# The last cast and the output store, moved from VectorE and SyncE to ScalarE

## The chip, the cores and the metric

The kernel runs on one core of a Trainium2 chip. The metric is device time in microseconds (us). The profile also gives a span, from the first to the last instruction of the program; it is about 1.8 us shorter than the time (1327.8 against 1329.5 us in the profiled run of the kernel before).

Lengths below a tenth of a microsecond are read from the records of single instructions, semaphore updates and DMA packets in the trace. The views round to 0.01 us, and the span to 0.1 us.

## The reference, cut to what matters

```
def reference(A_x, A_k_cache, A_v_cache, A_wq, A_wo, B_x, B_w1, ..., gate_w):
    # A: one decode step of attention, B=2, H=32, Sk=16384, Dh=128, all bf16
    q = (x @ wq) ...; scores = einsum(q, k_cache) * Dh**-0.5
    o = einsum(softmax(scores), v_cache);  a = o @ wo          # wo: 4096 x 1024
    # B: a small MLP on the same two rows
    b = x1 + gelu(layernorm(x1) @ w3) @ w4
    g = sigmoid((x * gate_w).sum(-1, keepdims=True))
    return g * a + (1 - g) * b                                 # 2 x 1 x 1024, bf16
```

The two caches are 537 MB; the result is 4 KB. The last thing that can happen is the product with `wo`, then the rounding of the sum to bf16, then the store.

## The kernel before

SyncE's queue carries every load of cache and weights. The last weight, `A_wo`, is cut into seven pieces, the last ones small, so that little work is left after the last byte. The sums of both halves of the model collect in one tile of PSUM (the memory that matmuls write to), `out_acc`.

```
    WO_SPLIT = [8, 8, 8, 4, 2, 1, 1]
    ...
    load_x()                          # two small loads, the only DMAs on ScalarE's queue
    ...
    wo = load_pieces(next_slot(), 0, A_wo, WO_SPLIT, ...)      # R.sync.dma_start, 7 pieces
    ...
    st_down(w4)
    wo_stage(wo)                      # matmuls into out_acc, piece by piece
    rows = t_tile([P, QW], BF16)
    R.vector.tensor_copy(out=rows, in_=out_acc)
    R.sync.dma_start(
        out=out.rearrange("b s (g n) -> g (b s) n", g=NQ),
        in_=rows[0 : P : APART, :],
        lane=(row_in[0], 32),
    )
    ...
    with tc.tile_critical(sync_engine=mybir.EngineType.Activation):
        R.emit([op for op in R.ops[:first_part] if op is not None])
        ...                           # the loops over the heads
        R.emit([op for op in R.ops[first_part:] if op is not None])
        nc.sync.wait_ge(row_in[0], 32)
```

`R` records operations and works out the semaphores between engines; all that it emits has the helper's line, L82, in the profile. The program must wait until the store has landed (`wait_ge`). And the section that holds the whole program is closed by one engine, named by `sync_engine`: here ScalarE ("Activation").

Of the kernel before, what the change touches and what calls it, by code (L numbers as in the profile page):

```python
# [184 lines left out]
def kernel(  # L185
# [15 lines left out]
    nc = tc.nc  # L201
# [19 lines left out]
    R = Order(nc, tc)  # L221
# [43 lines left out]
    def t_tile(shape, dtype, n=None):  # L265

        if n is None:
            n = t_next[0] % 2
            t_next[0] += 1
        flat = t_bufs[n][:]  # L270
        if dtype != FP32:
            flat = flat.bitcast(dtype)
        return shaped(flat, shape)
# [23 lines left out]
    def load_pieces(t, c0, weights, split, lanes, waits=()):  # L297
# [22 lines left out]
        out=perm[:].rearrange("k (h a) -> k h a", a=4),  # L320
        in_=ident_f[:].rearrange("k (a h) -> k h a", a=4),
# [23 lines left out]
    for g in range(1, 4):  # L345
        R.vector.tensor_tensor(
            out=osel_f, in0=osel_f, in1=ident_f[:, 40 * g : 40 * g + 8], op=ALU.add
# [9 lines left out]
        out=pick[:], in_=ident_f[:].rearrange("p (g w) -> p g w", w=32)[:, :, 0:B]  # L357
# [275 lines left out]
    out_acc = acc_ps[:, 0:QW]  # L633
# [203 lines left out]
    row_in = [tc.alloc_semaphore(f"row_in{n}") for n in range(2)]  # L837
# [33 lines left out]
    for k in range(LAST + 1):  # L871
# [19 lines left out]
    st_down(w4)  # L891
    wo_stage(wo)
    rows = t_tile([P, QW], BF16)
    R.vector.tensor_copy(out=rows, in_=out_acc)
    R.sync.dma_start(
        out=out.rearrange("b s (g n) -> g (b s) n", g=NQ),
        in_=rows[0 : P : APART, :],
        lane=(row_in[0], 32),
# [24 lines left out]
    def pe_loop():  # L923
        pe = nc.tensor
        got = Count(pe, sem["to_pe"])

        def scores(t):
            for m in range(NM):
                for v in range(4):
                    ins = score(pe, m, v)  # L930
                    if v == 0:
                        got.next(ins)
                    if v == 3:
                        ins.then_inc(sem["to_dve"], 1)

        def outputs(t):
            take(pe, v_in[t], 16)
            for m in range(NM):
                for g in range(4):
                    ins = weigh(pe, v_slot[t], m, g)  # L940
                    if m == 0 and g == 0:
                        ins.then_inc(sem["to_pool"], 1)
            ins.then_inc(sem["to_dve"], 1)
            got.next(join_heads(pe)).then_inc(sem["to_dve"], 1)

        def softmax(t):
            got.next(sum_rows(pe, mall, mdiag)).then_inc(sem["to_dve"], 1)
            got.next(sum_rows(pe, tot, stat["rs2"][:])).then_inc(sem["to_dve"], 1)
            take(pe, sem["from_pool"], 1)

        with pe.Fori(0, LAST + 1, NBIG) as k:
            loop_body(pe, k < LAST, scores, outputs, softmax, got.take_off)

    def dve_loop():
        dve = nc.vector
        counts = got, mine, exp_done = [
            Count(dve, sem[n]) for n in ("to_dve", "own_dve", "from_act")
        ]

        def scores(t):  # L960
            take(dve, k_in[t], 16)
            for m in range(NM):
                ins = turn_k(dve, k_slot[t + 1], m)
                if m >= 2:
                    got.next(ins)
                ins.then_inc(sem["to_pe"], 1)
            got.skip(1)
            got.next(top(dve)).then_inc(sem["own_dve"], 1)
            mine.next().then_inc(sem["free"], 1)

        def outputs(t):
            got.next(pick_head(dve, 0)).then_inc(sem["own_dve"], 1)
            for x in range(1, 4):
                mine.next(pick_head(dve, x)).then_inc(sem["own_dve"] if x < 3 else sem["to_pe"], 1)
            got.next(put_head(dve, bass.DynSlice(place + G * t, G))).then_inc(sem["free"], 1)

        def softmax(t):
            spread_top(dve).then_inc(sem["to_pe"], 1)
            got.next(head_top(dve, 0))
            head_top(dve, 1).then_inc(sem["own_dve"], 1)  # L980
            mine.next(bias(dve)).then_inc(sem["to_act"], 1)
            exp_done.next(turn_p(dve))
            split_sums(dve).then_inc(sem["to_pe"], 1)
            got.next(invert(dve))

        def take_off():
            for c in counts:
                if c.n:
                    c.take_off()

        with dve.Fori(0, G * (LAST + 1), G * NBIG) as place:
            loop_body(dve, place < G * LAST, scores, outputs, softmax, take_off)
# [17 lines left out]
    def act_steps():  # L1010
        for k in range(LAST + 1):
            exps(nc.scalar)._wait_ge(sem["to_act"], k + 1).then_inc(sem["from_act"], 1)

    def pool_steps():
        for k in range(LAST + 1):
            build_z(nc.gpsimd, min(k + 2, NT - 1))._wait_ge(sem["to_pool"], k + 1).then_inc(
                sem["from_pool"], 1
            )

    def meet(value):  # L1020
        for e in COMPUTE:
            getattr(nc, e).drain().then_inc(sem["met"], 1)
        for e in COMPUTE:
            getattr(nc, e).wait_ge(sem["met"], value)

    R.resolve()
    with tc.tile_critical(sync_engine=mybir.EngineType.Activation):
        R.emit([op for op in R.ops[:first_part] if op is not None])
        meet(len(COMPUTE))
        pe_loop()  # L1030
        dve_loop()
        act_steps()
        pool_steps()
        meet(2 * len(COMPUTE))
        R.emit([op for op in R.ops[first_part:] if op is not None])
        nc.sync.wait_ge(row_in[0], 32)


# [28 lines left out]
```

## Time and profile before

| | before |
|---|---|
| median time at first, 3 runs | 1329.58 us (1329.50 to 1329.78) |
| span of the profiled run | 1327.8 us |
| bytes read from HBM, mean rate | 572.5 MB, 431 GB/s |
| busy PE, DVE, ACT | 60%, 57%, 2% |
| last DMA of `A_wo` to the end of the span | about 4 us |

These lines are from the page of the kernel before. A digit of the DMA row is the mean busy share of the 16 DMA engines in one fortieth of the span, in tenths; 9 is 90% or more. The HBM line closes the list of DMA queues.

```profile
DMA  9999999999999999999999999999999999999998
...
HBM read 572.53 MB, written 0.00 MB: 431 GB/s over the span
```

The DMA engines are full from the first slice to the last but one. No compute engine is above 60%. So the time is that of the stream.

The next lines end the chain of work that ended last, in order of time (start, length, what).

```profile
1279.52 44.26 DMA slot<-in_A_wo_dram
1323.78 0.04 issue
1323.83 0.42 PE out_acc L82 x3
1324.27 0.42 DVE T L82
```

The chain sits on the transfer of `A_wo` for 44 us, and leaves it only for three matmuls and the cast. What follows is the tail that the change touches. The timeline of the kernel before shows it (start, length, engine, operation; in brackets, idle time of the engine before and what ended it):

```profile
1323.83 0.39 PE L82 MATMUL out_acc<-slot,T 128*17 128x256 bf16 x4 [0.23 <-DMA slot<-in_A_wo_dram]
1324.27 0.42 DVE L82 CAST T<-out_acc 128x256 bf16<-128x256 f32 x1 [16.30 <-PE out_acc L82]
1324.72 0.70 SPq L82 DMA_DIRECT2D out_dram<-T  x1
```

And the waits of SyncE's queue, where L1027 is the close of the program:

```profile
SPq L1027 <- DMA out_dram<-T: 1.0, 1, 1.0
```

The last matmuls end at 1324.2, the cast at 1324.7, the issue of the store at 1325.4, and SyncE waits 1.0 us for the landing. The rest to 1327.75 is closing synchronisation. In this document the **tail** is from the start of the cast to the end of the span, 3.48 us, and the **close** is its last part, from the landing of the store (the last update of its semaphore) to the end of the span, 1.29 us.

### The profile page before, as it was taken

Reading aid. Unit: us, or ns where it says so; the run is one execution under the profiler, and the core shown is the slowest. Engines: PE = TensorE matmul, PEld = TensorE weight load, DVE = VectorE, ACT = ScalarE, POOL = GpSimd, SP = SyncE. Lnnn points to the kernel's source line nnn. Section 1 sums busy time; section 2 is a strip of 40 time slices with the busy share of each in tenths; the row PEclk is TensorE's granted clock in tenths of the full one; section 3 lists DMA queues with packets and bytes.
Section 4 is the critical chain, followed back from the end, with each engine's and each line's share of the span. In section 5 each row is a group of like instructions: output and inputs, shape, how many; then the busy total and the mean of one; then the engine's idle time right before and its main releaser. Section 6 shows DMA issues by size and latency. Waiting matters only on the chain. (4 is left out here: it accounts for less than half of the span.)

```text
span 1327.8 us, 11371 instructions
## 1 busy us (share of the span) xinstructions
PE 801.6 (60%) x4806; PEld 305.4 (23%) x4859; DVE 762.7 (57%) x1009; ACT 27.2 (2%) x68; POOL 13.2 (1%) x41
## 2 busy tenths in 40 slices
PE   2767766555566655555765555576655557665553
PEld 1212222122222222222221222222222222222222
DVE  2277676655557665555666555566655556665540
ACT  0000000000000000000000000000000000000000
POOL 0000000000000000000000000000000000000000
PEclk9698887777888877778887777888777788877776
DMA  9999999999999999999999999999999999999998
GB/s 406 443 431 429 433 439 432 434 428 442 432 434 428 442 430 436 428 442 426 438 430 441 426 440 430 440 426 436 434 440 426 436 434 440 426 436 434 440 419 357
DMA packets 11118, 572.70 MB, mean 431 GB/s; under 512 B 1239, under 2 KB 1247, under 8 KB 1634
## 3 DMA queue, kind: packets, MB, share of 16 engines
q1 hardware_dynamic: 11100, 572.53, 99.6%
q8 instruction: 8, 0.13, 0.0%
q14 instruction: 4, 0.03, 0.0%
q10 hardware_dynamic: 6, 0.01, 0.0%
HBM read 572.53 MB, written 0.00 MB: 431 GB/s over the span
## 5 line engine op out<-in xcount | busy, mean ns | idle before, releaser
L526 PE MATMUL S<-T,z 128*128 128x512 bf16 x1933 | 571.6, 426 | 310.7 <-DVE T L517 298.8
L517 DVE STREAM_TRANSPOSE T<-slot 128x1024 f32<-128x1024 f32 x496 | 593.2, 1229 | 247.6 <-DVEq L921 196.0
L526 PEld LDWEIGHTS S<-T,z 128*128 128x128 bf16 x1984 | 171.1, 104 | 698.0 <-DVE T L517 532.5
L577 PE MATMUL O<-slot,PT 128*32 128x512 bf16 x2048 | 119.6, 387 | 7.2 <-PEq L921 7.2
L577 PEld LDWEIGHTS O<-slot,PT 128*32 128x32 bf16 x2048 | 74.0, 140 | 52.2 <-issue 23.0
L588 DVE TENSOR_SCALAR mix<-O,xmask 128x128 f32<-128x128 f32 x32 | 11.2, 351 | 103.6 <-PE O L577 103.6
L543 PE MATMUL tot<-rs,ones_f 128*128 128x2 f32 x62 | 18.2, 363 | 76.4 <-DVE rs L568 76.4
L560 ACT ACTIVATE mix<-S,nb 128x512 bf16<-128x512 f32 x31 | 21.3, 687 | 1158.3 <-DVE nb L550 1158.3
L596 PE MATMUL oc<-asel,mix 128*128 128x2 f32 x64 | 12.3, 262 | 51.8 <-DVE mix L591 51.8
L535 DVE TENSOR_REDUCE m<-S 128x1 f32<-128x512 f32 x31 | 21.4, 691 | 36.3 <-PE S L526 36.3
L565 DVE STREAM_TRANSPOSE PT<-mix 128x512 bf16<-128x512 bf16 x31 | 22.0, 711 | 26.2 <-ACT mix L560 26.2
L591 DVE SCALAR_TENSOR_TENSOR mix<-O,xmask,mix 128x128 f32<-128x128 f32 x96 | 33.7, 351 | 3.4
L543 PEld LDWEIGHTS tot<-rs,ones_f 128*128 128x128 f32 x62 | 15.5, 311 | 82.3 <-DVE rs L568 82.3
L543 PE MATMUL mall<-mix,ones_f 128*128 128x128 f32 x62 | 15.1, 326 | 16.3 <-DVE mix L538 16.3
L596 PEld LDWEIGHTS oc<-asel,mix 128*128 128x128 f32 x64 | 9.5, 188 | 66.2 <-DVE mix L591 66.2
L547 DVE TENSOR_REDUCE mx<-mall 64x1 f32<-64x64 f32 x62 | 13.8, 222 | 18.4 <-PE mall L543 18.0
L82 PE MATMUL out_acc<-slot,T 128*17 128x256 bf16 x240 | 12.1, 361 | 17.1 <-DMA slot<-in_A_wo_dram 9.3
L508 POOL TENSOR_TENSOR z<-qsel,own 128x32 bf16<-128x32 bf16 x31 | 10.5, 340 | 1167.3 <-PE O L577 1167.3
L82 PE MATMUL S<-T,z 128*128 128x512 bf16 x62 | 17.9, 416 | 6.3 <-DVE T L82 5.9
L82 DVE STREAM_TRANSPOSE T<-slot 128x1024 f32<-128x1024 f32 x16 | 19.1, 1228 | 1.6 <-PE S L82 1.3
L573 DVE RECIPROCAL rinv<-tot 128x2 f32<-128x2 f32 x31 | 5.3, 170 | 21.1 <-PE tot L543 21.1
L599 DVE TENSOR_TENSOR OT<-oc,rinv 128x2 f32 x32 | 5.1, 159 | 15.2 <-PE oc L596 15.2
(115 smaller groups left out, 129.5 us busy)
## 6 DMA issues: line engine op xcount, KB each, us to landing
slot<-in_B_w_dram SPq DMA_DIRECT2D x1, 7168.0 KB, 48.5
slot<-in_B_w_dram SPq DMA_DIRECT2D x2, 3584.0 KB, 28.4
slot<-in_A_wo_dram SPq DMA_DIRECT2D x3, 2048.0 KB, 37.2
slot<-in_B_w_dram SPq DMA_DIRECT2D x2, 2048.0 KB, 29.2
slot<-in_A_wo_dram SPq DMA_DIRECT2D x1, 1024.0 KB, 43.5
slot<-in_A_k_cache_dram SPq DMA_DIRECT2D x32, 49.3
slot<-in_A_v_cache_dram SPq DMA_DIRECT2D x32, 35.1
slot<-in_A_wo_dram SPq DMA_DIRECT2D x1, 512.0 KB, 44.3
```

The source lines that it names most:

```text
L82: op = Op(engine, lambda: getattr(eng, method)(*args, **kwargs), reads, writes, waits, lane)
L517: return vector.transpose(out=t_tile([P, 2, CJ, 32], FP32, m % 2).rearrange("p w j s -> p j w s"), in_=K[:].bitcast(FP32)[:, m * CW : (m + ...
L526: return tensor.matmul(S, lhsT=z[:, v, NM - 1 - m : NM - 1 - m + P], rhs=Tb[:, v // 2, :, v % 2], start=(m == 0 and v == 0), stop=(m == NM ...
L535: return vector.reduce_max(out=stat["m"][:], in_=S, axis=AX.X)
L543: return tensor.matmul(ps, lhsT=ones_f[:], rhs=src, start=True, stop=True)
L547: return vector.reduce_max(out=stat["mx"][pa, :], in_=mall[pa, pa], axis=AX.X)
L560: return scalar.activation(out=Pr, in_=S, func=ACTF.Exp, bias=stat["nb"][:], scale=scale, accum_out=stat["rs"][:])
L565: return vector.transpose(out=PT[:], in_=Pr)
L577: return tensor.matmul(O[32 * g : 32 * g + 32, :], lhsT=PT[:, m : CJ * 32 : 16], rhs=V[:].rearrange("p (j d) -> p j d", d=Dh)[:, j0 : j0 + ...
L588: return vector.tensor_scalar(out=Os, in0=Ox, scalar1=xmask[:, 0:1], scalar2=None, op0=ALU.mult)
L591: return vector.scalar_tensor_tensor(out=Os, in0=Ox, scalar=xmask[:, x : x + 1], in1=Os, op0=ALU.mult, op1=ALU.add)
L596: return tensor.matmul(oc, lhsT=Os, rhs=asel[:], start=True, stop=True)
```

## The change

Its intent: ScalarE is idle at the end, so it can cast, and it can then issue the store itself, with no hand-over to another engine, on its own ring of descriptors, in which nothing stands. (A ring is here the list of transfers that one issuing engine has handed to the DMA engines.) ScalarE also does the wait for the store.

```diff
-    R.vector.tensor_copy(out=rows, in_=out_acc)
-    R.sync.dma_start(
+    R.scalar.copy(out=rows, in_=out_acc)
+    R.scalar.dma_start(
         out=out.rearrange("b s (g n) -> g (b s) n", g=NQ),
         in_=rows[0 : P : APART, :],
         lane=(row_in[0], 32),
@@
-        nc.sync.wait_ge(row_in[0], 32)
+        nc.scalar.wait_ge(row_in[0], 32)
```

## The prediction

> **What bounds the kernel now.** The span is 1327.8 us (median time 1329.58 us, three runs within 0.3 us). The page's slices show the DMA engines at 9 tenths or more in 39 of 40, 431 GB/s in the mean; PE is busy 60%, DVE 57%, ACT 2%. The table by stage shows DMA shares of 0.96 to 1.03 up to 1320 us. The chain of waits that ended last is, at its end, the transfer of A_wo (44.26 us), three last matmuls (0.42 us), the cast. So the stream from HBM sets the time, and the change touches none of it: every load stays on SyncE's queue, in the same order. Only what follows the last piece of A_wo is exposed.
>
> **The exposed tail, before** (timeline):
> - 1323.83: last matmuls, ending 1324.24
> - 1324.27: VectorE cast of out_acc, 128x256, 0.42 us
> - 1324.72: SyncE issues the store (4 KB), 0.70 us
> - SyncE then waits 1.0 us for it to land (the DMA queue's own waits), to about 1326.4
> - 1.4 us of closing synchronisation, to 1327.8
>
> That is about 3.5 us, 0.26% of the span: the most that the change could save, and it replaces pieces of it by like pieces.
>
> **What the change moves.** By the compiled order of instructions, one copy and one DMA issue leave VectorE and SyncE and stand at the end of ScalarE's list; nothing else moves, and no table load is added.
>
> 1. Cast on ScalarE. The ScalarE groups by form show 128x512 from PSUM 687 ns, 128x56 249 ns, 128x2 172 ns. A line through the first and last gives about 0.43 us for 128x256 (estimate), against 0.42 us on VectorE: difference 0.0 us, at most 0.1 either way. ScalarE has been idle since 1278.7.
> 2. Hand-overs. VectorE to SyncE took 0.03 us. ScalarE to its own queue still needs a semaphore wait, so 0.03 to 0.1 us.
> 3. The issue. SyncE took 0.70 us for the store; ScalarE's two issues at the start took 0.54 and 0.23 us. I expect 0.5 to 0.7 us: 0 to 0.2 us saved.
> 4. The "otherwise empty ring". SyncE's ring is empty here too: the A_wo pieces had landed before the last matmuls, and the DMA share is 0.00 after 1324. There is nothing to get past. The Trainium skill, "DMA: Bandwidth & Descriptors", section "Queues, rings and completion order", says that SP and ACT each own one ring on each of the same 16 engines, not engines of their own; landing should take the same 1.0 us after the issue.
> 5. The end. ScalarE collects the other engines at the close, so having it wait for the store may save one hop, 0.05 to 0.2 us (estimate from the 0.03 to 0.05 us hand-overs in the timeline).
>
> Sum: 0 to 0.4 us saved, about 0.15, or 0.01%: inside the spread of three runs.
>
> **Prediction:** 1329.4 us, 8 in 10 between 1328.4 and 1330.6. Faster by over 2%: 0.01; within 2%: 0.98; slower by over 2%: 0.01.
>
> **What the profile would show.** Right: the ScalarE copy 0.40 to 0.50 us, beginning 0.02 to 0.06 us after the last matmul; the store issued in 0.5 to 0.7 us from the ACT queue; about 1 us to landing; the last A_wo piece at the same moment within 1 us. Wrong: a ScalarE copy over 0.6 us, a pause over 0.2 us before the copy or the issue, or a new table load.
>
> **What would make it wrong.** Drift of the HBM rate by 0.1% is 1.3 us, more than the whole change. [...]

## The result, and the profile after

| | before | after |
|---|---|---|
| median time, 6 runs each | 1329.61 us (1329.36 to 1329.78) | 1329.66 us (1329.51 to 1329.90) |
| ratio | | 1.0001, 95% interval 0.9988 to 1.0014 |
| span of the profiled run | 1327.75 us | 1327.82 us |
| tail, of it close | 3.482, 1.291 us | 3.629, 1.479 us |

Ratios here and below are the mean time of one kernel's runs over that of the other's runs of the same rounds, so they are not quite the ratios of the medians quoted.

The lines of the page after that answer to those shown before. They say the same of the stream:

```profile
DMA  9999999999999999999999999999999999999998
...
HBM read 572.53 MB, written 0.00 MB: 431 GB/s over the span
```

The end of the chain after the change:

```profile
1279.83 43.88 DMA slot<-in_A_wo_dram
1323.70 0.04 issue
1323.75 0.42 PE out_acc L82 x4
1324.19 0.37 ACT T L82
```

The tail in the timeline after the change:

```profile
1323.75 0.39 PE L82 MATMUL out_acc<-slot,T 128*17 128x256 bf16 x4 [0.21 <-DMA slot<-in_A_wo_dram]
1324.19 0.37 ACT L82 CAST T<-out_acc 128x256 bf16<-128x256 f32 x1 [45.20 <-PE out_acc L82]
1324.59 0.65 ACTq L82 DMA_DIRECT2D out_dram<-T  x1
```

Each step did get a little shorter: the cast 0.42 to 0.37 us, the issue 0.70 to 0.65 us. The issue ended at 1325.24, where it had ended at 1325.42. Yet the span did not get shorter. The waits of SyncE's queue after the change show something new at L1027:

```profile
SPq L1027 <- ACTq L1027: 39.1, 1, 39.1
...
SPq L1062 <- ACTq L1027: 0.2, 1, 0.2
```

SyncE, which now has nothing to do after its last load, waits 39 us for ScalarE's queue, at the close. The records of the queues' own instructions, as times from the span's start, show the difference. SEM is a wait on or an update of semaphores, DRAIN an engine's report that it is done. The time of an instruction is its start.

```
before                                     after
1295.699 ScalarE SEM: opens the close
1326.459 store landed                      1326.342 store landed
1326.476 SyncE has seen it                 1326.363 ScalarE has seen it
                                           1326.519 ScalarE SEM: opens the close for all engines
                                           1326.56-1326.61 all five engines DRAIN
1326.642 SyncE DRAIN (the last to report)  1326.693 ScalarE SEM: gathers two of them
1326.672 ScalarE SEM: gathers it           1326.775 ScalarE SEM: gathers the other two
1326.749 ScalarE closes                    1326.851 ScalarE closes
1327.750 end of the span                   1327.821 end of the span
```

Before the change ScalarE had long opened the close, since it had nothing left to do; PE's report ended at 1324.28 and VectorE's at 1324.74. When the store landed, only SyncE's report was missing. After the change nobody could report before the store had landed, because the engine that opens the close was the one that waited for it. From landing to "ScalarE closes" it took 0.29 us before and 0.51 us after. From there to the end it took 1.00 and 0.97 us, so 0.03 us of these 0.22 us came back.

That is a reading of two traces. The experiments test it.

### The profile page after: what moved, and what is told of

Same layout as the page of the kernel before. It is cut to its first block, busy times and chain, and to the rows that moved or that the text cites. A ratio compares the mean times of both kernels' runs of the same rounds, so it can differ in the third digit from the quotient of the medians.

```text
span 1327.8 us, 11371 instructions
## 1 busy us (share of the span) xinstructions
PE 805.5 (61%) x4806; PEld 306.8 (23%) x4859; DVE 762.6 (57%) x1008; ACT 27.6 (2%) x69; POOL 13.3 (1%) x41
## 3 DMA queue, kind: packets, MB, share of 16 engines
q1 hardware_dynamic: 11088, 572.53, 99.6%
HBM read 572.53 MB, written 0.00 MB: 431 GB/s over the span
```

## The experiments

**Theory.** The stream sets the time. In the tail the change gains about 0.05 us in the cast, and loses 0.19 us because the engine that opens the close now waits for the store. The issue is 0.05 us shorter too, but that brings no earlier landing: from the start of the issue to the landing it took 1.740 us before and 1.748 us after. **Rival A:** a store is completed or reported later in ScalarE's queue. **Rival B:** waiting and branching on ScalarE is slower by itself. The ring's state plays no part in theory or rivals, since SyncE's ring too is empty by then; two more experiments ask what it would take for it to play one.

### 1. SyncE waits for ScalarE's store

```diff
 # from the changed kernel
-        nc.scalar.wait_ge(row_in[0], 32)
+        nc.sync.wait_ge(row_in[0], 32)
```

> The changed kernel, but SyncE, not ScalarE, waits for the store to land. Tail = from the start of the final cast to the end of the span; it was 3.48 us before the change and 3.63 after it. Theory (ScalarE opens the closing synchronisation, so a ScalarE that waits for the store makes all others start late): landing 2.15 us after the cast's start as after the change, close from landing to the end 1.29 us as before it, tail 3.44. Rival A (ScalarE's queue completes or reports a store later): tail stays 3.63. Time on the clock outside the trace: 1329.5, not to be told from either kernel.

Measured: landed 2.126 us after the cast's start, close 1.293 us, tail 3.419 us. Median 1329.46 us, 5 runs, against 1329.57 us of the kernel before, 9 runs; ratio 0.9999, 0.9985 to 1.0013. The close is back to its old length with the store still in ScalarE's queue, so rival A falls: the store is not reported later there. The long wait of SyncE's queue at L1027 is now for the store itself:

```profile
SPq L1027 <- DMA out_dram<-T: 38.9, 1, 38.9
```

### 2. and 3. Another engine opens the close

```diff
 # 2: from the changed kernel; 3: from the kernel before
-    with tc.tile_critical(sync_engine=mybir.EngineType.Activation):
+    with tc.tile_critical(sync_engine=mybir.EngineType.SP):
```

> The changed kernel, ScalarE waits for the store, but SyncE is the engine that opens and gathers the close. Theory: close from landing to the end shrinks from 1.48 to about 1.29 us, tail 3.44 us. Rival B (a wait and branch on ScalarE is slower by itself): close stays 1.48 us, tail 3.63.

> The kernel before the change, with SyncE as the engine that opens and gathers the close. Theory: SyncE now waits for the store and opens the close, so the close grows from 1.29 to about 1.48 us without any use of ScalarE; tail from 3.48 to about 3.67 us. Rivals A and B: tail stays 3.48.

Measured, 2: close 1.228 us (0.06 us below what was expected), tail 3.361 us; median 1329.38 us, 4 runs, ratio 0.9998, 0.9982 to 1.0013. Measured, 3: close 1.457 us, tail 3.656 us; median 1329.68 us, 4 runs, ratio 1.0001, 0.9985 to 1.0016. Both were timed against the kernel before, 1329.57 us.

This is the pair that decides. With SyncE as the opener, the kernel before gets the long close though ScalarE neither casts, stores nor waits for the store, and the changed kernel gets the short one though ScalarE still waits. Rival B predicted the opposite in both. The waits of SyncE's queue in experiment 2 show it as opener, first held by PE's matmuls, then by ScalarE alone:

```profile
SPq L1027 <- PEq L1027: 36.6, 1, 36.6
...
SPq L1027 <- ACTq L1027: 2.3, 1, 2.3
```

The 2.3 us are ScalarE's last work: cast, issue and landing. All others had reported before. In experiment 3 the wait for the store looks as it did in the kernel before; only the opener differs:

```profile
SPq L1027 <- DMA out_dram<-T: 1.0, 1, 1.0
```

From the landing to the record with which the opener closes it took 0.28 us in experiment 2 and 0.50 us in experiment 3.

### 4. and 5. Each half of the change alone

```diff
 # 4, from the kernel before
-    R.vector.tensor_copy(out=rows, in_=out_acc)
+    R.scalar.copy(out=rows, in_=out_acc)
```

```diff
 # 5, from the kernel before
-    R.sync.dma_start(
+    R.scalar.dma_start(
         out=out.rearrange("b s (g n) -> g (b s) n", g=NQ),
@@
-        nc.sync.wait_ge(row_in[0], 32)
+        nc.scalar.wait_ge(row_in[0], 32)
```

> Only the cast is moved to ScalarE; SyncE issues the store and waits for it. Theory: cast 0.37 us instead of 0.42, issue 0.70 us as before, close 1.29 us as before; tail 3.43 to 3.46 us. If the hand-over from ScalarE to SyncE costs more than the 0.03 us seen from VectorE, tail 3.48 or more.

> Only the store and the wait for it are moved to ScalarE; VectorE casts. Theory: cast 0.42 us, issue 0.65 us instead of 0.70, close 1.48 us instead of 1.29; tail 3.60 to 3.68 us, the slowest tail of the four combinations.

Measured, 4: tail 3.412 us, 0.02 us below the range expected; median 1329.49 us, 4 runs, ratio 0.9999, 0.9984 to 1.0015. Measured, 5: tail 3.674 us; median 1329.62 us, 4 runs, against 1329.52 us, 7 runs; ratio 1.0000, 0.9984 to 1.0017. The timelines of the two, experiment 4 first:

```profile
1324.21 0.37 ACT L82 CAST T<-out_acc 128x256 bf16<-128x256 f32 x1 [45.50 <-PE out_acc L82]
1324.61 0.69 SPq L82 DMA_DIRECT2D out_dram<-T  x1
```

```profile
1324.17 0.42 DVE L82 CAST T<-out_acc 128x256 bf16<-128x256 f32 x1 [16.34 <-PE out_acc L82]
1324.62 0.64 ACTq L82 DMA_DIRECT2D out_dram<-T  x1
```

A hand-over cost about the same here whether it crossed engines or not: cast's end to issue's start took 0.027 us from VectorE to SyncE (before), 0.025 us from ScalarE to SyncE (4), 0.032 us from VectorE to ScalarE (5), 0.030 us from ScalarE to its own queue (after). Nothing was to be saved there.

### 6. and 7. A ring with something in it

```diff
 # 6: from the kernel before; 7: the same in the changed kernel
+    R.sync.dma_start(            # 8 MB that nobody needs, behind the last piece of A_wo
+        out=v_slot[NBIG - 1][:].rearrange("p (j d) -> p j d", d=Dh),
+        in_=cache_rows(A_k_cache, 0),
+        waits=[(sem["met"], 2 * len(COMPUTE))],
+        lane=(busy, 16),
+        untracked=True,
+    )
     st_down(w4)
     wo_stage(wo)
@@
+        nc.sync.wait_ge(busy, 16)
```

> The kernel before the change, with an extra 8 MB load that nobody needs queued on SyncE behind the last A_wo piece, so that SyncE's ring is not empty when the store is issued. Theory (a ring only matters when something stands in it): the store lands only when the extra load has drained, 8.39 MB at 431 GB/s = 19.5 us after the last A_wo piece; from issue to landing about 19 to 20 us instead of 1.7. Time 1329.6 + 18 to 20 = 1348 to 1350. Rival (rings do not delay each other's or their own entries by much): store lands 2 to 4 us after its issue.

> The changed kernel with the same extra 8 MB load on SyncE. Theory: ScalarE's ring is empty, its packets take turns with the load's, and the store lands 2 to 5 us after its issue, 15 us or more earlier than with the store behind the load. The whole time is set by the extra load in both, 1346 to 1350, so it tells little.

Measured, 6: the store landed 18.40 us after its issue began, where it took 1.74 us before. Median 1346.28 us, 4 runs, against 1329.52 us; ratio 1.0125, 1.0108 to 1.0142. The time is below the 1348 to 1350 expected because the extra load begins to move early: its first packets start at 1322.14 us, before the old tail begins. Only the mechanism was expected rightly. Measured, 7: the store landed 11.24 us after its issue began, 7.2 us earlier than in 6, but far from the 2 to 5 us expected. Median 1346.17 us, ratio 1.0124, 1.0107 to 1.0141; as expected, the extra load sets the end in both, and the time tells nothing.

So the intent of the change holds for the landing of the store where a ring is full: behind 8 MB the store waits, and on the other ring it overtakes. No run here shows a gain in time from it. What was missed in 7 is the size of a turn. The store has three packets on each of four DMA engines. On one of them these started at 1329.176, 1331.614 and 4 bytes more at 1334.051 us, 2.44 us apart. (The kept trace does not name a packet's engine; the twelve packets fall into four such rows of equal steps.) A packet of the load is 64 KB and takes 2.42 us. The Trainium skill, "DMA: Bandwidth & Descriptors", section "Queues, rings and completion order", says that each DMA engine takes turns between the rings "at *packet* granularity". This trace agrees: one packet of the load between each two of the store.

### 8. Half of the last weight

```diff
 # from the changed kernel; wrong result on purpose; the list of semaphores is cut to match
-    WO_SPLIT = [8, 8, 8, 4, 2, 1, 1]
+    WO_SPLIT = [8, 4, 2, 1, 1]
@@
-        for r in range(32):
+        for r in range(16):
```

> The changed kernel with only half of A_wo loaded and used (4.19 MB less; the result is wrong on purpose). Theory (the stream from HBM sets the time, and the tail follows it one to one): 4.19 MB at 431 GB/s = 9.7 us less, time 1319.9, tail still 3.6 us. Rival (the tail or an engine's work sets the end): change under 3 us.

Measured: median 1320.28 us, 4 runs, against 1329.52 us of the kernel before; ratio 0.9932, 0.9916 to 0.9949. The cast started at 1314.44 us, 9.75 us earlier than the 1324.19 us of the changed kernel; 4.19 MB at 431 GB/s are 9.73 us. The bytes read fell from 572.53 to 568.33 MB:

```profile
HBM read 568.33 MB, written 0.00 MB: 431 GB/s over the span
```

That settles what bounds the kernel: bytes taken from the stream bring its end forward one to one. (Half of the matmuls with `A_wo` went too, but in the kernel before PE stood idle before each of these pieces until its DMA had landed.) The time fell by a little less, 9.24 us, in part because of the tail. The tail was 3.82 us, 0.2 us longer than expected: the close took 1.693 us, because SyncE passed its next wait of the close 0.42 us after its report, where it took 0.09 us in the changed kernel. From the landing to "ScalarE closes" it was 0.51 us here too. Why SyncE was late in this run is open. (The comparison with the reference did not notice the missing half; this is no claim that the result is right.)

### 9. and 10. Smaller packets, and the changed kernel again

```diff
 # 9, from experiment 7: rows of 4 KB instead of 64 KB
-        in_=cache_rows(A_k_cache, 0),
+        in_=A_k_cache[0, 0:G].rearrange("a s d -> (a s) d").rearrange(
+            "(j p r) d -> p j (r d)", p=P, r=16
+        ),
```

The destination is written in the same shape.

> The changed kernel with the extra 8 MB load on SyncE, as in the run before of that kind, but with the load's rows cut to 4 KB (16 rows of 4 KB for each partition instead of one of 64 KB). There the store, alone on ScalarE's ring, took 11.2 us from issue to landing: its packets on one engine stood 2.44 us apart, one 64 KB packet (2.42 us) of the load between each two. Theory (the rings take turns packet by packet, so the store waits for the size of the other ring's packet): with 4 KB packets a turn takes about 2.42/16 = 0.15 us, the store lands 1.8 to 4 us after its issue. Rival (the store waits for a share of the bytes queued, whatever the packets): still about 11 us.

> The changed kernel itself, once more, to see how far the tail repeats: cast 0.37 us, issue 0.64 to 0.65, landing 2.12 to 2.15 us after the cast's start, close 1.46 to 1.48 us, tail 3.60 to 3.63. If the close came out at 1.3 or at 1.7 us, the difference between 1.29 and 1.48 us would be no more than scatter.

Measured, 9 (one execution): the store landed 4.63 us after its issue began. The turns are confirmed: its packets on one engine started at 1328.664, 1328.843 and 1329.021 us, 0.18 us apart, and a 4 KB packet of the load takes 0.159 us. But 4.63 us is above the 4 us expected. The first packet of the store started 3.27 us after the end of the issue, as it started 3.78 us after it in experiment 7, against 0.64 us with empty rings. With packets 16 times smaller this first delay fell only by 0.5 us, and turns alone do not explain it; it is open.

Measured, 10 (one execution): cast 0.373, issue 0.644, landed 2.136 us after the cast's start, close 1.479 us, tail 3.615 us. The tail repeats to about 0.01 us.

### The tails side by side

| kernel | cast | issue and ring | waits for the store | opens the close | cast start to landing | close | tail |
|---|---|---|---|---|---|---|---|
| before | VectorE | SyncE | SyncE | ScalarE | 2.191 | 1.291 | 3.482 |
| 4 | ScalarE | SyncE | SyncE | ScalarE | 2.132 | 1.280 | 3.412 |
| 1 | ScalarE | ScalarE | SyncE | ScalarE | 2.126 | 1.293 | 3.419 |
| 2 | ScalarE | ScalarE | ScalarE | SyncE | 2.133 | 1.228 | 3.361 |
| after | ScalarE | ScalarE | ScalarE | ScalarE | 2.150 | 1.479 | 3.629 |
| after, again | ScalarE | ScalarE | ScalarE | ScalarE | 2.136 | 1.479 | 3.615 |
| 5 | VectorE | ScalarE | ScalarE | ScalarE | 2.196 | 1.478 | 3.674 |
| 3 | VectorE | SyncE | SyncE | SyncE | 2.199 | 1.457 | 3.656 |

Where the waiter is not the opener, the close is 1.23 to 1.29 us; where it is, 1.46 to 1.48 us. Experiment 8, of the second kind, is not in the table: its close was 1.69 us, and one such stray trace is as large as the difference itself. The part of the close that the theory speaks of, from the landing to the opener's closing record, does not stray: it is 0.28 to 0.29 us in before, 1, 2 and 4, and 0.50 to 0.51 us in after (twice), 3, 5 and 8. Which engine casts moves the landing by 0.05 to 0.06 us (before against 4, after against 5). Which ring carries the store moves it by less than 0.02 us (4 against 1, before against 5).

Experiment 2 has the shortest tail, 0.12 us shorter than before. Its median is 0.19 us under that of the kernel before, but 0.12 us in 1329 us is less than a hundredth of a per cent, and the interval of its ratio holds 1. No run here shows on the clock that it beats the kernel before.

## Why the prediction was right or wrong

The time was right: 1329.66 us measured, 1329.4 us predicted, inside 1328.4 to 1330.6, and "within 2%" had 0.98. The range was 2.2 us wide and the change in the tail 0.15 us, so the time could hardly miss. It was right for the main reason given: the stream sets the time (experiment 8), and the change only replaces pieces of a tail of 3.5 us by like pieces. Point by point:

1. **Cast.** Predicted 0.43 us, "0.40 to 0.50"; measured 0.372 us in the changed kernel, outside that window by 0.03 us. The line was drawn through ScalarE's ACTIVATE records, and the copy is recorded as another operation, CAST, for which that line does not hold. Right that the difference from VectorE would be under 0.1 us: it is 0.05 us.
2. **Hand-over.** Predicted 0.03 to 0.1 us, no gain; measured 0.030 us against 0.027 us. Right.
3. **Issue.** Predicted 0.5 to 0.7 us; measured 0.645 against 0.696 us. Right in length, but the "0 to 0.2 us saved" came out as none: the first packet of the store started 1.30 us after the start of the issue before and 1.29 us after, and the landing followed 1.740 and 1.748 us after that start.
4. **The ring.** Predicted that nothing stood in SyncE's ring either, and that the landing would take the same 1.0 us after the issue. Measured 1.10 against 1.04 us, and from the start of the issue 1.748 against 1.740 us. Right; experiment 6 shows that a ring with something in it would have delayed the landing by 16.7 us. The whole way of 1.74 us is near the 2.0 us of fixed cost that the Trainium skill, "DMA: Bandwidth & Descriptors", section "Anatomy of one DMA — SWDGE (gpsimd) path", gives for another issue path, which no run here uses.
5. **The end.** Predicted that having ScalarE, which collects the others, wait for the store "may save one hop, 0.05 to 0.2 us". This step failed, in sign: the close grew from 1.291 to 1.479 us, by 0.19 us. The prediction saw that ScalarE gathers the close, but not that it also opens it. An opener that waits holds up all reports; experiments 2 and 3 show this from both sides.

So the sum was "0 to 0.4 us saved, about 0.15", and the tail lost 0.15 us (3.482 to 3.629 us): 0.19 us lost in the close, 0.04 us gained from the start of the cast to the landing. An error of 0.3 us in 1330 us cannot be seen in the time, and a right time is no proof of each of its terms.

## What to carry to other kernels

Before moving work at the end of a kernel that streams from HBM, measure the tail from the start of the first piece that moves: it bounds what the move can give, here 3.48 us or 0.26% of the span. In these runs an empty ring brought the store an earlier landing only where the other ring was full at that moment, and even then the other ring's packets set the length of each turn: 2.42 us for 64 KB, 0.16 us for 4 KB. Let the engine that opens the closing synchronisation be one that has nothing left to wait for; here that is worth 0.2 us in the trace and cannot be seen in the time.

## What the Trainium skill lacked or had wrong

- No page tells that in a program's own closing synchronisation the engine that opens it had better not be the last one at work. The close took 1.23 to 1.29 us where another engine waited for the last store, and 1.46 to 1.48 us where the opener did (1.69 us in experiment 8). "Runtime: NRT & Kernel Launch" speaks of barriers around a kernel only.
- "DMA: Bandwidth & Descriptors", section "Issuing engines are not separate DMA queues", calls the sequencer's time to issue a DMA usually small relative to the DMA itself. For the 4 KB store it was 0.64 to 0.70 us of the 1.72 to 1.75 us from issue to landing, so over a third.
- The same page, section "Queues, rings and completion order", has the turns between rings by packet, as seen here, but not what that costs a small DMA beside a large one: 11.24 us from issue to landing beside packets of 64 KB, 4.63 us beside 4 KB, 1.74 us alone. The first delay in the two (3.3 to 3.8 us) is not explained by it.
